# First MoE of a fused attention and two-MoE kernel: products a and b of eight slices by seven products per 2x2 blocks, g by HBM, first output as a stage of its own

## The chip, the cores and the metric

The kernel runs on one core of a Trainium2 chip. The metric is the device time of one execution in microseconds (us). Engines are called TensorE, VectorE, ScalarE, GpSimd and SyncE; profile rows abbreviate them as PE (PEld for its weight loads), DVE, ACT, POOL and SP.

## What is computed

Attention without softmax, over 4 batches, 8 heads, 576 positions and 64 dimensions, then two MLPs over the 2304 tokens. Inputs of the MLPs' weights are float64.

```python
kv = einsum('bhsd,bhse->bhde', k, v)
o = einsum('bhsd,bhde->bhse', q, kv)
x = o / sqrt(mean(o * o, -1) + 1e-6) * g_norm          # as x: [2304, 512]
a, b = x @ w_a, x @ w_b                                # [512, 1536] each
x = (a * b) @ w_out                                    # [1536, 512]
h = x @ w_in                                           # [512, 1024]
sm = softmax(h); solu = h * sm
out = (layernorm(solu) * g_ln) @ w_out2                # [1024, 512]
```

## The kernel before

Every large matrix product is made of three TensorE matmuls in the type fp32r: a value is split into a high part and a low part (the rest), and high x high, high x low and low x high are summed in PSUM. `three` (L778 to L781) issues these for a, b and the last output. A float64 weight chunk of 128 x 512 comes in as integer bits, and `decode` (L328) makes a high and a low float from it: one operation on ScalarE (L339), five on VectorE (L342 to L360), then in `store` a cast on ScalarE (L441), a subtraction (L442) and a sum (L443) on GpSimd.

The kernel is written as a program that runs its own clock: the class `Order` holds for each engine when it comes free, each operation has an assumed duration, and the main loop at the end takes at each point the TensorE work that is ready. The order of the instructions on every engine, SyncE's DMA queue included, comes out of this and is fixed when the kernel is built. All DMAs are issued by SyncE and wait there in that order.

Attention (`att_kv`, `att_1`, `att_2`, `att_hop`) makes 18 tiles of 128 tokens of x, transposed and split into xh and xl. Tiles 0 to 11 are transposed by TensorE, tiles 12 to 17 by VectorE and a trip through HBM. Between its pieces TensorE already works on the first MoE.

The first MoE goes slice by slice: 1536 hidden units are 12 slices f of 128. For each slice and each block of tokens (`BLOCKS`: 384, 384, 512, 512, 512; `EARLY` for slice 0, with two blocks of 256) `ab_items` issues 24 matmuls (a and b, four pieces of the 512 inputs, three matmuls each), ScalarE copies a out of PSUM (L833), VectorE multiplies (L834), and the product g is split (L835, L836). `y_items` then multiplies g with that slice of w_out (12 matmuls a block, L864), and the result is added into ya in SBUF on VectorE (L877; for slice 0 copied by ScalarE, L875). A weight stays in SBUF from its decode to its last use.

The second MoE's first product h is made of seven products for each 2x2 blocks instead of eight (`run_h`, `SEQ`): sums of blocks of w_in (`sums`) and of ya (`make_a`) are formed, and the seven results are combined in PSUM. Six of the seven operand pairs of one half of w_in go to HBM and come back (`late_loads`) when xh and xl are no longer needed. The softmax, the norm and the last output follow (`post_h`, `run_t`, `run_o`). SBUF comes from tile pools that are opened and released as stages end; PSUM has three pairs of banks for the MoE and two single banks for attention, which become a fourth pair when it ends.

Of the kernel before, what the change touches and what calls it, by code (L numbers as in the profile page):

```python
# [26 lines left out]
NB = 384  # L27
BLOCKS = [(0, 384), (384, 384), (768, 512), (1280, 512), (1792, 512)]
NBLK = len(BLOCKS)
EARLY = [(0, 384), (384, 256), (640, 256), (896, 384), (1280, 512), (1792, 512)]  # L30


def blocks_of(f):
    return EARLY if f < 1 else BLOCKS

HALVES = [1280, 1024]
NTT = NT // P
SC = 4
CH = 512

# [11 lines left out]
class Order:  # L52

    def __init__(self):
        self.now, self.events, self.seq = 0.0, [], 0
        self.free = {"A": 0.0, "V": 0.0, "G": 0.0}
        self.pool = 0.0
        self.end, self.cold = 0.0, 3.6  # L60
        self.dma = 1.68

    def chain(self, ops, rank=0, t=None):


# [3 lines left out]
    def until(self, t):  # L69

        while self.events and self.events[0][0] <= t:
            due, rank, seq, i, ops = heapq.heappop(self.events)
            eng, dur, fn = ops[i]
            both = eng == "S"
# [22 lines left out]
    def soon(self, eng, t, rank):  # L97

        for due, r, _, i, ops in self.events:
            if r > min(rank - 0.4, 1):  # L100
                continue
            for e, dur, _ in ops[i:i + 4]:
                if due >= t + self.AHEAD[eng]:
                    break
                if e and (e == eng or e == "S" and eng in "VG"):
                    return True
# [15 lines left out]
    def wait(self):  # L122

        assert self.events, "nothing left that anything could wait for"
        self.now = max(self.now, self.events[0][0])
        self.until(self.now)

# [7 lines left out]

# [15 lines left out]

@with_exitstack
def attention_moe_moe_kernel(ctx: ExitStack, tc, kv_in, kv_tail, q_in, g_norm, w1, w_in, w_out2, g_ln, out):
# [4 lines left out]
    INF = float("inf")  # L158

    cst = ctx.enter_context(tc.tile_pool(name="cst", bufs=1, side="left"))  # L160
    xs = ctx.enter_context(tc.tile_pool(name="xs", bufs=1, side="left"))
    wp = ctx.enter_context(tc.tile_pool(name="wp", bufs=6, side="right"))
    psm = ctx.enter_context(tc.tile_pool(name="psm", bufs=1, space=bass.MemoryType.PSUM))

    ctx.enter_context(tc.manual_schedule())

    att = tc.alloc_tile_pool(name="att", bufs=2, side="left")
    psa = tc.alloc_tile_pool(name="psa", bufs=2, space=bass.MemoryType.PSUM)
    yp = tc.alloc_tile_pool(name="yp", bufs=1, side="right")
    ph1 = tc.alloc_tile_pool(name="ph1", bufs=2, side="right")  # L170
    dr = ctx.enter_context(tc.tile_pool(name="dr", bufs=1, space=bass.MemoryType.DRAM))
    w2 = ph2 = psx = None
# [4 lines left out]
    ps_free = {0: 0.0, 1: 0.0, 2: 0.0}  # L177
    att_left = [NTT]
    started = set()

    def ps_ready():
        return min(ps_free.values())

    def ps_tile(nm):
        i = min(ps_free, key=ps_free.get)
        assert ps_free[i] < INF
        ps_free[i] = INF
        pool = psx if i == 3 else psm
        return i, pool.tile([P, 2, 512], F32, tag=f"ps{i}", name=nm)

    def ps_done(i):
        def done(t):
            ps_free[i] = t

        return (None, 0, done)


    ident = cst.tile([P, P], F32, tag="ident", name="ident")
    gn = cst.tile([P, 1], F32, tag="gn", name="gn")
    gl_sb = cst.tile([P, NF2], F32, tag="gln", name="gln")  # L200
# [1210 lines left out]
```

## Time and profile before

| | |
|---|---|
| median of 3 runs | 686.88 us (686.8 to 687.05) |
| span of the profiled execution, first to last instruction | 685.0 us |
| the profiled execution's own time | not recorded apart from its span |
| TensorE (PE) busy | 671.6 us, 98% |
| VectorE (DVE) busy | 515.3 us, 75% |
| ScalarE (ACT), GpSimd (POOL) busy | 278.8 and 279.0 us, 41% each |
| moved by DMA | 82.42 MB, mean 120 GB/s |

Matmuls are pipelined: one of 512 columns is listed with some 390 ns from its start to its end, while the next starts some 230 ns after it. So listed lengths of matmuls must not be added up; what a stream costs is read from the distance of starts, or from the merged stretches in the chain of work that ended last, which counts each stretch of time once. For the other engines the listed length of an operation is what it holds the engine. "x12" is a count, "idle before" is the time for which the engine had stood still.

### The profile page before, as it was taken

The numbers are of one execution on the slowest core, as the hardware profiler recorded it, in microseconds if no ns is written. First come the engines' busy times: TensorE is split into PE (matmuls) and PEld (weight loads), VectorE is DVE, ScalarE is ACT, GpSimd is POOL, SyncE is SP. The second block draws the span as 40 slices with busy tenths as digits, with TensorE's granted clock in tenths as the row PEclk, the third lists the DMA queues.
The fourth block names the chain that finished last, engine by engine and source line by source line (L and its number), as shares of the span: only waits on it lengthen the run. The fifth ranks groups of instructions, "written<-read, shape, count | busy, mean of one in ns | idle before, by whom it ended". The sixth has DMA issues, their size and how long they took to land.

```text
span 685.0 us, 9642 instructions
## 1 busy us (share of the span) xinstructions
PE 671.6 (98%) x3566; PEld 585.4 (85%) x3566; DVE 515.3 (75%) x752; ACT 278.8 (41%) x485; POOL 279.0 (41%) x280
## 2 busy tenths in 40 slices
PE   5999999999999999999999999999999999999998
PEld 4899988989898898989898988889787888888887
DVE  2987955888987899788888888655569969787640
ACT  3877434333233232322323323212257566654431
POOL 1669614242365454533224141311457667552010
PEclk9999999999999999999999999999999999999999
DMA  9983621122233121023041321113413564633451
GB/s 328 375 282 108 191 71 62 62 96 89 93 125 121 62 92 62 32 92 124 32 149 66 115 101 62 63 61 125 173 72 105 146 176 119 198 114 105 138 177 47
DMA packets 63694, 82.42 MB, mean 120 GB/s; under 512 B 6176, under 2 KB 45344, under 8 KB 63648
## 3 DMA queue, kind: packets, MB, share of 16 engines
q1 hardware_dynamic: 63648, 81.81, 36.0%
q8 instruction: 28, 0.46, 0.3%
q14 instruction: 18, 0.15, 0.1%
HBM read 59.25 MB, written 22.54 MB: 119 GB/s over the span
## 4 chain that ended last, share of the span: by engine, by line
PE 95%; DMA 2%; DVE 1%; SPq 1%; issue 0%; ACT 0%; ACTq 0%
PE y L864 21%; PE ab L779 15%; PE ab L781 15%; PE ab L780 14%; PE h L1027 12%; PE out L781 5%; PE out L780 5%; PE out L779 5%; PE o L657 2%; DMA kv<-in_kv 1%; DMA q<-in_q 1%; PE pkv L612 1%; PE t L756 1%; SPq L282 0%; DVE ya L877 0%
## 5 line engine op out<-in xcount | busy, mean ns | idle before, releaser
L779 PE MATMUL ab<-xh,wh_w 128*128 128x512 f32 (+2 forms) x488 | 179.5, 368 | 0.2 <-DVE ya L877 0.2
L781 PE MATMUL ab<-xh,wl_w 128*128 128x512 f32 (+2 forms) x488 | 178.4, 366 | 0.0
L780 PE MATMUL ab<-xl,wh_w 128*128 128x512 f32 (+2 forms) x488 | 178.3, 365 | 0.0
L877 DVE TENSOR_TENSOR ya<-y,ya 128x1024 f32<-128x1024 f32 (+1 forms) x110 | 122.2, 1111 | 2.7 <-PE y L864 2.5
L833 ACT COPY a<-ab 128x512 f32<-128x512 f32 (+2 forms) x61 | 32.8, 538 | 191.2 <-PE ab L781 191.2
L442 POOL TENSOR_TENSOR f_w<-f_w,wh_w 128x512 f32<-128x512 f32 x34 | 45.4, 1335 | 158.6 <-ACT wh_w L441 100.8
L779 PEld LDWEIGHTS ab<-xh,wh_w 128*128 128x128 f32 x488 | 91.8, 188 | 12.2 <-DVE ya L877 0.5
L834 DVE TENSOR_TENSOR ab<-ab,a 128x512 f32<-128x512 f32 (+2 forms) x61 | 38.8, 637 | 83.2 <-ACT a L833 83.0
L780 PEld LDWEIGHTS ab<-xl,wh_w 128*128 128x128 f32 x488 | 91.7, 188 | 11.3
L781 PEld LDWEIGHTS ab<-xh,wl_w 128*128 128x128 f32 x488 | 91.7, 188 | 10.9
L864 PE MATMUL y<-gl,wh_w 128*128 128x512 f32 (+2 forms) x244 | 89.2, 366 | 0.3 <-DVE gl L836 0.3
L864 PE MATMUL y<-gh,wh_w 128*128 128x512 f32 (+2 forms) x244 | 89.2, 366 | 0.0
L864 PE MATMUL y<-gh,wl_w 128*128 128x512 f32 (+2 forms) x244 | 89.2, 366 | 0.0
L1027 PE MATMUL h<-wd,lateh 128*128 128x512 f32 x216 | 58.0, 389 | 0.0
L443 POOL TENSOR_TENSOR wl_w<-f_w,u_w 128x512 fp32r<-128x512 f32 x36 | 47.1, 1312 | 16.0 <-DVE f_w L442 12.3
L864 PEld LDWEIGHTS y<-gl,wh_w 128*128 128x128 f32 x244 | 45.8, 188 | 6.4 <-DVE gl L836 0.7
L864 PEld LDWEIGHTS y<-gh,wh_w 128*128 128x128 f32 x244 | 45.9, 188 | 5.8 <-issue 0.2
L864 PEld LDWEIGHTS y<-gh,wl_w 128*128 128x128 f32 x244 | 45.8, 188 | 5.4
L1027 PEld LDWEIGHTS h<-wd,lateh 128*128 128x128 f32 x216 | 40.6, 188 | 8.4
L1027 PE MATMUL h<-latel,lateh 128*128 128x512 f32 x162 | 45.8, 391 | 0.7 <-ACT bt L1054 0.7
L957 POOL TENSOR_TENSOR lateh<-ya,lateh 128x512 fp32r<-128x512 f32 (+1 forms) x18 | 19.7, 1105 | 63.6 <-ACT lateh L956 63.5
L780 PE MATMUL out<-wl_o,dh 128*128 128x512 f32 (+1 forms) x114 | 43.1, 378 | 0.0
(118 smaller groups left out, 1155.1 us busy)
## 6 DMA issues: line engine op xcount, KB each, us to landing
raw_w<-in_w SPq DMA_DIRECT2D x36, 512.0 KB, 3.4
su<-ya SPq DMA_DIRECT2D x34, 256.0 KB, 2.7
kv<-in_kv SPq DMA_DIRECT2D x16, 512.0 KB, 7.6
ya<-su SPq DMA_DIRECT2D x32, 256.0 KB, 3.1
out<-ot SPq DMA_DIRECT2D x17, 256.0 KB, 2.1
raw_i<-in_w_in SPq DMA_DIRECT2D x8, 512.0 KB, 3.4
raw_o<-in_w_out SPq DMA_DIRECT2D x8, 512.0 KB, 3.2
so<-raw_o SPq DMA_DIRECT2D x8, 512.0 KB, 2.8
```

Source lines behind the costliest of these rows:

```text
L442: ("S" if k[1] == 0 and k[2] < 2 else "T", 0.62 if k[1] == 0 and k[2] < 2 else 1.32, lambda: (nc.vector if k[1] == 0 and k[2] < 2 else nc. ...
L443: ("T", 1.38, lambda: nc.gpsimd.tensor_tensor(out=lo, in0=f, in1=u, op=ALU.add)),
L657: nc.tensor.matmul(ps[m * w:(m + 1) * w, p * P:(p + 1) * P], lhsT=src[:, m * w:(m + 1) * w], rhs=bds[b % 2][:, p], start=True, stop=True)
L779: nc.tensor.matmul(o, lhsT=ah, rhs=bh, start=first, stop=False)
L780: nc.tensor.matmul(o, lhsT=ah, rhs=bl, start=False, stop=False)
L781: nc.tensor.matmul(o, lhsT=al, rhs=bh, start=False, stop=last)
L833: ("A", 0.45 * k, lambda: nc.scalar.copy(out=a, in_=ps[:, 0, 0:nb])),
L834: ("V", 0.54 * k, lambda: nc.vector.tensor_tensor(out=g, in0=g, in1=a, op=ALU.mult)),
L864: nc.tensor.matmul(o, lhsT=x[:, s], rhs=y, start=f == fs[0] and n == 0, stop=f == fs[-1] and n == 2)
L877: op = ("V", 0.9 * nb / NB, lambda: nc.vector.tensor_tensor(out=dst, in0=src, in1=dst, op=ALU.add))
L957: ("G", 2.15 * cost, lambda: nc.gpsimd.tensor_tensor(out=lo[:, n], in0=src, in1=hi[:, n].bitcast(F32), op=ALU.subtract)),
L1027: nc.tensor.matmul(o, lhsT=x, rhs=y, start=first and k == m == 0, stop=k == 1 and m == 2, skip_group_check=not first)
```

## The change

- a and b: slices 0 and 1 as before, but in blocks of 384 tokens. The others are taken in pairs of slices and pairs of blocks (`step_items`): seven products of 256 x 256 hidden-and-input blocks for a and seven for b, each of 6 matmuls of 384 columns, with sums of x blocks (`x_sum_of`) and of weight blocks (`sums_w`), and additions in and behind PSUM. The pair of slices 2 and 3 is done plainly, but in the same frame (`plain_step`, `PLAIN_STEPS`). These steps begin when all tiles of x are there. TensorE picks the first ready one of the next four products (`LOOK`).
- Weights of the pairs are split and stored to HBM as soon as they are decoded (`to_hbm`), and each group is loaded into its one fixed place when its predecessor there has been used last (`w_fill`). Slices of w_out go to HBM too and are loaded when the blocks of x in their place are used up.
- g is stored to HBM unsplit (`store_g`), 72 stores.
- The first output is a stage of its own behind all of a and b (`c_items`): for each block of tokens g is loaded (60 loads), split by ScalarE and VectorE, and all 12 slices are summed in PSUM; ScalarE copies the sum to ya. The additions at L877 are gone.
- The operands of w_in need no trip to HBM any more; w_in and w_out2 are decoded in the first output's stage.
- Some splits and sums may run on VectorE or GpSimd ("X"), whichever the build-time clock has free.
- SBUF is laid out by fixed addresses (`Map`) in place of pools, and PSUM is taken by single banks in the pair steps.

```diff
+TB = 384
+NTB = NT // TB
+PLAIN = 2
...
+            if eng == "X":
+                can = [e for e in "VG" if self.free[e] <= due + 0.01 and not self.soon(e, due, rank)]
...
+class Map:
+    XB, T0, R2, W, DEC, STG, WS, AB, CST = 0, 73728, 92160, 137216, 165888, 186368, 194560, 202752, 211968
...
+    def to_hbm(key, n, fill, then, t, rank=5):
...
+                d = w_hbm[key] = dr.tile([P, 2, n], F32, tag="hb_" + "_".join(map(str, key)), name="hb_" + "_".join(map(str, key)))
+                nc.sync.dma_start(out=d, in_=tile_.bitcast(F32))
...
+                return [
+                    add(a[:, 0:h], w1_[:, 0:h], w1_[:, h:], ALU.add), add(a[:, h:], a[:, 0:h], w0[:, 0:h], ALU.subtract),
+                    (None, 0, group(1, a, part)),
+                    add(b[:, 0:h], w0[:, 0:h], w1_[:, 0:h], ALU.subtract), add(b[:, h:], w0[:, h:], a[:, h:], ALU.subtract),
...
+    PLAIN_STEPS = {(1, 0), (1, 1), (1, 2)}
...
+    def w_fill():
+        seen = set()
+        for key in list(w_next):
+            _, m, g = key
+            at = m, (0, 1, 2, 3, 2)[g]
+            if at not in seen and slot_free.get(at, INF) <= od.now and w_in_hbm.get(key, INF) <= od.now:
+                o = wt[m][at[1]]
+                nc.sync.dma_start(out=(o if g < 4 else o[:, :, 0:CH // 2]).bitcast(F32), in_=w_hbm[key])
...
+    def store_g(f, j, s):
...
+            nc.sync.dma_start(out=g_hbm[f][:, j * TB:(j + 1) * TB], in_=g_t[s])
...
+    def x_sum_of(t):
...
+            return ("V", 0.95, lambda: nc.vector.tensor_tensor(out=o, in0=a, in1=b, op=op))
+        def both(n, src):
+            hi, lo = b12 if n == T4 else [a[t][:, (T1, T2, T3).index(n)] for a in (th, tl)]
+            return [("A", 0.82, lambda: nc.scalar.copy(out=hi, in_=src)), add(lo, src, hi, ALU.subtract),
...
+                add(t1, b21[0], t2, ALU.subtract), add(t1, t1, b21[1], ALU.add), *both(T4, t1),
+                add(t2, t2, b11[0], ALU.subtract), add(t2, t2, b11[1], ALU.subtract), *both(T3, t2)], rank=rank, t=w)
...
+            add(t1, b12[0], b11[0], ALU.subtract), add(t1, t1, b12[1], ALU.add), add(t1, t1, b11[1], ALU.subtract),
+            *both(T1, t1), add(t2, b22[0], t1, ALU.subtract), add(t2, t2, b22[1], ALU.add), *both(T2, t2), (None, 0, rest),
...
+    WSEQ = [("P1", 0, 0, B11), ("P6", 1, 1, T2), ("P2", 0, 1, B21), ("P5", 1, 0, T1), ("P7", 2, 0, T3),
+            ("P3", 2, 1, B22), ("P4", 3, 0, T4)]
...
+        def item(m, name, g, c, n):
...
+                else:
+                    w = max(w, st.get({"P2": "s1", "P7": "u2", "P3": "s5", "P4": "v"}[name], INF))
...
+                for k in range(2):
+                    sl = slice(c * 256 + k * P, c * 256 + (k + 1) * P)
+                    w = wt[m][g]
+                    three(o, w[:, 0, sl], w[:, 1, sl], x[2 * k], x[2 * k + 1], first and k == 0, k == 1, not first)
...
+        return [item(m, *p) for p in WSEQ for m in range(2)]
...
+    c_units = [(j, f) for j in range(NBLK) for f in range(NF1)]
...
-                if f < 1:
-                    op = ("A", 0.75 * nb / NB, lambda: nc.scalar.copy(out=dst, in_=src))
-                else:
-                    op = ("V", 0.9 * nb / NB, lambda: nc.vector.tensor_tensor(out=dst, in0=src, in1=dst, op=ALU.add))
...
+    ab = [[ab_items(f, j) for j in range(NTB)] for f in range(PLAIN)]
+    steps = [(plain_step if (fp, t) in PLAIN_STEPS else step_items)(fp, t) for fp in range(PLAIN // 2, NF1 // 2) for t in range(NTB // 2)]
+    b_items = [x for s in steps for x in s]
+    ATT, LOOK = 2.0, 4
...
+        if not plain and not att_left[0] and b_items:
+            n = next((n for n, x in enumerate(b_items[0:LOOK]) if x[1]() <= od.now), None)
...
+        if len(b_items) < 3 and c_items and c_items[0][1]() <= od.now:
```

## Rows read from the trace of the kernel before

**Rows 1.** The page's busy shares, and the chain's shares by line.
```profile
PE 671.6 (98%) x3566; PEld 585.4 (85%) x3566; DVE 515.3 (75%) x752; ACT 278.8 (41%) x485; POOL 279.0 (41%) x280
by line: PE y L864 21.0%; PE ab L779 14.6%; PE ab L781 14.5%; PE ab L780 14.5%; PE h L1027 12.3%; PE out L781 4.8%; PE out L780 4.8%; PE out L779 4.8%; PE o L657 2.5%; DMA kv<-in_kv 1.2%; DMA q<-in_q 1.1%; PE pkv L612 0.8%; PE t L756 0.6%; 
```

**Rows 2.** Busy time by stage: stretch, length, engines in the order PE to POOL, clock, DMA.
```profile
12.30:30.00 17.70, 16.49 (x185) 14.79 (x186) 14.22 (x26) 12.86 (x29) 10.84 (x7) 1.00 1.05 383
30.00:93.00 63.00, 62.78 (x547) 59.25 (x546) 54.06 (x105) 41.40 (x85) 39.88 (x27) 1.00 0.61 202
93.00:496.00 403.00, 402.67 (x1938) 353.82 (x1937) 314.37 (x446) 121.69 (x216) 142.78 (x110) 1.00 0.25 87
496.00:685.00 189.00, 185.06 (x842) 153.84 (x840) 129.00 (x170) 99.61 (x148) 84.78 (x129) 1.00 0.43 128
130.00:325.00 195.00, 195.00 (x948) 172.51 (x947) 166.95 (x232) 60.42 (x108) 85.98 (x65) 1.00 0.26 92
```

**Rows 3.** Chain pieces of TensorE (start, us): 512, 512, 384 columns; counts of two forms.
```profile
118.25 2.72 PE y L864 x12
125.15 2.76 PE y L864 x12
139.66 2.10 PE y L864 x12
...
L779 PE MATMUL ab<-xh,wh_w 128*128 128x512 f32 x280 | 109.2, 390 | 0.2 <-DVE ya L877 0.2
L779 PE MATMUL ab<-xh,wh_w 128*128 128x384 f32 x192 | 65.3, 340 | 0.0
```

**Rows 4.** TensorE's groups by form in 0 to 93 us, first line of three.
```profile
L779 PE MATMUL ab<-xh,wh_w 128*128 128x384 f32 x32 | 11.6, 362 | 0.0
L779 PE MATMUL ab<-xh,wh_w 128*128 128x512 f32 x16 | 6.5, 404 | 0.2 <-DVE ya L877 0.2
L864 PE MATMUL y<-gh,wh_w 128*128 128x384 f32 x16 | 5.5, 346 | 0.0
L779 PE MATMUL ab<-xh,wh_w 128*128 128x256 f32 x16 | 5.1, 316 | 0.0
L864 PE MATMUL y<-gh,wh_w 128*128 128x256 f32 x8 | 2.4, 295 | 0.0
```

**Rows 5.** VectorE's last operation on x tiles: ns min/median/max, first and last start.
```profile
L736 DVE SCALAR_TENSOR_TENSOR xl<-ya,gn,xh x24: 326/342/353, 74.3 to 92.2; 128x128 fp32r<-128x128 f32 x24
```

**Rows 6.** DMA issues: count, KB each, median us to landing.
```profile
kv<-in_kv SPq DMA_DIRECT2D x16, 512.0 KB, 7.6
si<-wd SPq DMA_DIRECT2D x6, 512.0 KB, 2.6
latel<-si SPq DMA_DIRECT2D x6, 512.0 KB, 4.6
```

**Rows 7.** Operations by line, ns min/median/max; the last row as in rows 3.
```profile
L342 DVE TENSOR_SCALAR u_w<-u_w x36: 413/418/1509, 9.5 to 440.6; 128x512 f32<-128x512 f32 x36
L345 DVE TENSOR_SCALAR u_w<-u_w x36: 395/420/1471, 9.9 to 441.0; 128x512 uint32<-128x512 uint32 x36
L351 DVE SCALAR_TENSOR_TENSOR f_w<-raw_w,u_w x36: 639/682/1662, 10.4 to 441.5; 128x512 uint32<-128x512 uint32 x36
L356 DVE TENSOR_SCALAR u_w<-f_w x36: 378/417/1411, 11.1 to 442.2; 128x512 uint32<-128x512 uint32 x36
L360 DVE SCALAR_TENSOR_TENSOR u_w<-raw_w,u_w x36: 676/692/1781, 11.6 to 442.7; 128x512 f32<-128x512 uint32 x36
L442 DVE TENSOR_TENSOR f_w<-f_w,wh_w x2: 682/686/691, 12.9 to 21.4; 128x512 f32<-128x512 f32 x2
L443 POOL TENSOR_TENSOR wl_w<-f_w,u_w x36: 1267/1298/1580, 13.7 to 447.2; 128x512 fp32r<-128x512 f32 x36
L877 DVE TENSOR_TENSOR ya<-y,ya x110: 937/1212/1226, 75.4 to 495.9; 128x1024 f32<-128x1024 f32 x66, 128x768 f32<-128x768 f32 x44
L834 DVE TENSOR_TENSOR ab<-ab,a 128x384 f32<-128x384 f32 x24 | 13.5, 563 | 25.3 <-ACT a L833 25.2
```

More of the change, by code (lines that the diff above doesn't have):

```diff
@@ L450, in attention_moe_moe_kernel, with done @@
-    waiting, waiting_i = [], []
+        if x < PLAIN and y < 2:
+            at = wt[y][2 * x]
+            hi, lo = at[:, 0], at[:, 1]
+            def done(t):
+                w_ready["w", x, y] = t
+                free()
+            od.chain([
+                ("A", 0.58, lambda: nc.scalar.copy(out=hi, in_=f)),
+                ("X", (0.62, 1.32), lambda e: tt(e)(out=f, in0=f, in1=hi.bitcast(F32), op=ALU.subtract)),
+                ("T", 1.38, lambda: nc.gpsimd.tensor_tensor(out=lo, in0=f, in1=u, op=ALU.add)),
+                (None, 0, done),
+            ], rank=rank_of(k) - 0.01, t=t)
+            return
@@ new lines, in post, with x_sums @@
+            od.chain([(None, 0, when_ok((A_S, G_S), ops))], t=od.now + 0.62)
+            plain_done.add((f, j))
+        return [(COST[TB], lambda m=m, kt=kt: ready(m, kt), lambda m=m, kt=kt: run(m, kt)) for m in range(2) for kt in range(NP)]
+    x_sum = {}
+    sum_q = list(range(3))
+    SUM_RANK = (4.5, 4.6, 4.7)
+    def x_sums():
+        if len([1 for k in w_in_hbm if k[0] == PLAIN // 2]) < 6:
+            return
+        for t in list(sum_q):
+            if any(block_ready(j) > od.now for j in (2 * t, 2 * t + 1)):
+                continue
+            if t == 1 and kv_left[0] or t == 2 and att_left[0] or t and (t - 1, T3) not in x_sum:
+                continue
+            sum_q.remove(t)
+            x_sum_of(t)
@@ new lines, in attention_moe_moe_kernel, with c_loads @@
+    s_free = [0.0] * 4
+    steps_left = {}
+    GI, GS = Slots(6), Slots(3)
+    c_units = [(j, f) for j in range(NBLK) for f in range(NF1)]
+    c_load = list(c_units)
+    g_ready, wo_at = {}, {}
+    y_ready = {}
+    def c_loads():
+        for f in range(NF1):
+            t = f // 6
+            if f not in wo_at and steps_left.get((NF1 // 2 - 1, t)) == 0 and w_in_hbm.get(("wo", f), INF) <= od.now:
+                nc.sync.dma_start(out=wo[f].bitcast(F32), in_=w_hbm["wo", f])
+                wo_at[f] = od.load(8 * CH * P)
+        if any(steps_left.get((NF1 // 2 - 1, t)) != 0 for t in range(2)):
+            return
+        while c_load and GI.ok():
+            j, f = c_load[0]
+            t0, nb = BLOCKS[j]
+            if max(g_at.get((f, i), INF) for i in range(t0 // TB, (t0 + nb - 1) // TB + 1)) > od.now:
+                return
+            c_load.pop(0)
+            s = GI.take()
+            nc.sync.dma_start(out=gi_t[s][:, 0:nb], in_=g_hbm[f][:, t0:t0 + nb])
+            at = od.load(4 * nb * P)
+            c_wait.append((j, f, s, nb, at))
+            od.chain([(None, 0, c_split)], rank=0.5, t=at)
@@ new lines, in attention_moe_moe_kernel, with c_split, done @@
+    c_wait = []
+    def c_split(t):
+        while c_wait and GS.ok() and c_wait[0][4] <= t:
+            j, f, s, nb, _ = c_wait.pop(0)
+            sg = GS.take()
+            g, (gh, gl) = gi_t[s][:, 0:nb], [a[:, 0:nb] for a in gs_t[sg]]
+            k = nb / CH
+            def done(w, j=j, f=f, s=s, sg=sg, gh=gh, gl=gl):
+                GI.give(s)
+                g_ready[j, f] = (w, gh, gl, sg)
+            od.chain([
+                ("A", 0.08 + 0.5 * k, lambda g=g, gh=gh: nc.scalar.copy(out=gh, in_=g)),
+                ("V", 0.08 + 0.54 * k, lambda g=g, gh=gh, gl=gl: nc.vector.tensor_tensor(
+                    out=gl, in0=g, in1=gh.bitcast(F32), op=ALU.subtract)),
+                (None, 0, done),
+            ], rank=0.5, t=t)
@@ L979, in h_new @@
         i = todo_h[0] // 2 if todo_h else None
-        if i not in a_ops or sum(t <= od.now for t in ps_free.values()) < places or i - 1 not in z_done:
+        if i not in a_ops or sum(place_time(n) <= od.now for n in range(4)) < places or i - 1 not in z_done:
             return INF
@@ L1115, in go @@
             if i in ON_PE:
[L1116 removed]
+                to_pe = ot_t
                 minus = [("A", 1.15, lambda h=h: nc.scalar.activation(
@@ L1245, in next_ab @@
             return busy[0]
-        two = [f for f in range(NF1) if ab[f]][0:2]
+        two = [f for f in range(PLAIN) if ab[f]][0:2]
         for n, f in enumerate(two):
```

879 lines of the change are left out of this document (569 added, 310 removed).

## Prediction

> **What bounds the kernel now.** I read the page's busy shares first, then the table by stage, then the chain of work that ended last, and only then prices of single instructions. TensorE is busy 671.6 of 685.0 us [rows 1]. The reader is to see in the stage table that this is no average over unlike stages: from 30 us on TensorE is busy in 62.78 of 63.00, 402.67 of 403.00 and 185.06 of 189.00 us, with a granted clock of 1.00 (full speed, 2.4 GHz) [rows 2]. Of the 13.4 us that it is idle, about 8.9 lie before 30 us, where kv loads arrive, and 4 in the last stage. The chain agrees: a and b have 14.6 + 14.5 + 14.5 = 43.6% of it, y 21.0% [rows 1]. So only fewer or shorter matmuls can save much, and whatever else the change adds counts only where TensorE comes to wait for it.
>
> **TensorE: what goes.** Chain share times span is the present cost of a and b: 0.436 x 685.0 = 298.7 us. Piece by piece the same comes out. Twelve matmuls of 512 columns take 2.72 to 2.76 us (0.2267 to 0.230 each), twelve of 384 take 2.10 (0.175) [rows 3]; a 256 one, scaled by columns from the 384, is an estimated 0.117. a and b have 3 x 280, 3 x 192 and 3 x 16 of these [rows 3, 4]: 840 x 0.2283 + 576 x 0.175 + 48 x 0.117 = 298.2.
>
> After the change every a/b matmul has 384 columns. Slices 0 and 1, and the pair 2, 3 in all three of its steps, stay plain: 4 slices x 6 blocks x 24 matmuls = 576. The eight slices 4 to 11 are 4 pairs x 3 pairs of blocks x 14 products (seven for a, seven for b) x 6 matmuls = 1008, where 1152 would be plain. 1584 x 0.175 = 277.2 us. Gain: 298.7 - 277.2 = 21.5 us, and up to 24 at 0.1734, an estimate from the faster row of 512 columns less 128 columns at 2.4 GHz (0.2267 - 0.0533). So the change shortens 7/8 of two thirds of a and b, and gives almost nothing back by the narrower blocks: per column 0.456 ns against 0.446. The first output has 720 matmuls where y had 732: 432 x 0.2283 + 288 x 0.175 = 149.0 for 149.2 us, 0.2 less. h and the last output keep their matmuls.
>
> So TensorE's part alone: 685.0 - 21.5 - 0.2 = 663.3 us of span.
>
> **Attention stage (to 93 us).** The last x tile is written at about 92.5 us [rows 5]. Until then TensorE fills the gaps with 96 a/b matmuls of 384 columns, 46 of 512, 48 of 256, and 48 and 24 y matmuls of 384 and 256 (each row of [rows 4] stands for three lines of its kind): 16.8 + 10.5 + 5.6 + 8.4 + 2.8 = 44.1 us. After the change nothing but slices 0 and 1 may run there (no y, no pair step before the last tile), and their blocks 0 to 4: 10 x 24 x 0.175 = 42.0 us; block 5 waits for the last tile. That leaves 2.1 us uncovered: 0 if attention gets shorter by it, 5 if blocks arrive in lumps. I take 2.1.
>
> **Weights by HBM.** Before, a decoded weight stays in SBUF. Now each group of a pair, and each w_out slice, is stored and loaded again, all on SP's queue, with g beside it (72 stores, 60 loads). Bytes while a and b run: 22 MB weights out, 16 back, 14 of g out, 14 raw in: 66 MB in some 237 us, 280 GB/s; the queue reached 383 [rows 2]. A 512 KB store lands after 2.6 us, a load after 4.6, and a load in the saturated start after 7.6 [rows 6]. A step lasts 14 x 1.05 = 14.7 us, and a group's place is free some 8 to 9 us before its successor is needed (group 0: used in products 1 and 5 of the row of seven, needed at the next step's first). So I cost the reload at nothing; the cover is the remaining products of the step. Were a load to take 12 us, four changes of pair would wait about 3 us each: 12 us. Behind a waiting store on SP stand the other stores and these loads.
>
> **VectorE and GpSimd (93 to about 330 us).** Removed: 110 adds into ya (122 us in all, 0.95 to 1.22 each [rows 7]); in their place 10 copies on ScalarE. Added and kept, by the medians of [rows 7]:
> - 28 of the 36 weight decodes (eight done by then; the code's limit for the attention stage is nine) x (0.418 + 0.420 + 0.682 + 0.417 + 0.692 = 2.63) = 74 us, and 28 joins on GpSimd x 1.30 = 36
> - sums of x: 3 x 13 operations of 768 columns with both inputs in SBUF; the nearest row has 512 columns and 0.686, so 1.03 each, 40 us
> - weight splits and sums, where 256 columns count half of 512: 8 x (3 x 0.686 + 5 x 0.343) + 2 x (0.686 + 2 x 0.343) + 12 x 0.686 = 41 us if all on VectorE, twice that on GpSimd (1.30 against 0.686)
> - 12 steps x 10 additions and products x 0.563 = 68, plain ones 14 x 0.563 = 8
>
> That is 231 us of 237 if GpSimd takes none of the 41, 190 (80%) if it takes all. VectorE at 167 of 195 us (86%) held TensorE up nowhere in 130 to 325 us [rows 2], so pressure of this size is bearable. But the place of a wait is new. Within a step a's products need each other's evictions: product 4 of the seven waits for an addition on VectorE that waits for product 7, with three other products between the two, 3.15 us; less 0.563 for the addition and an estimated 0.4 for hand-overs that is some 2.2 us of slack. A VectorE operation in the way costs 0.4 to 1.0, or 1.5 to 1.8 at its longest. Bounds for the twelve steps: 0 (slack never used up) to 12 us (1 us each). I take 1.5 in all, nearer to the row without waits.
>
> One thing speaks against this. Among the rows the decode operations on SBUF show medians of 0.418 and 0.692 but longest cases of 1.509 and 1.781, while the ya adds, which have one input in PSUM, never pass 1.226 [rows 7]; the excess is about one GpSimd operation. The Trainium skill (SBUF — State Buffer, "SBUF: two separate sides") says that VectorE operations with two SBUF inputs or in a fast mode share a port pair with GpSimd under an exclusive lock, the later one blocked for the whole instruction. The trace agrees, and the sums of x are of the blocked kind where the ya adds were not; what that gives is the first rival.
>
> **Hand-overs.** The first output begins only when the products are through; its g loads and w_out loads are released one step (14.7 us) earlier, against 4.6 us a load. The second MoE's weights are decoded during 149 us of first output, their sums stay in SBUF now. Its second A operand waits for the last first-output unit, then GpSimd's four sums of 256 columns and splits of 3.5 x 512, (2 + 3.5) x 1.30 = 7.2 us [rows 7], under 14 x 3 x 0.2283 = 9.6 us of the first pair. I cost both at nothing, with 0 to 3 us each in the range.
>
> **Sum.** 663.3 + 2.1 + 1.5 = 666.9 us of span. The median of the runs stands 686.88 - 685.0 = 1.9 above the profiled span; the change leaves what lies around the span alone: 668.8, forecast **669**.
>
> **Rivals.**
> 1. The lock and the load together: sums and decodes on VectorE cannot run beside GpSimd. 231 + 36 = 267 us in a row would be 30 too many. Against it, 76 us of VectorE's work reads PSUM and can lie beside GpSimd, and 40 us (w_out's decodes and splits) may slip into the first output. So I let 40% of the 30 reach TensorE, 12 us: **681**, between 675 and 685. It shows as TensorE waiting for weight loads whose stores waited for the joins. Chance 0.19.
> 2. Slower: the product chain of a step is exposed. The price is one wait per step at products 4 and 7. A gain of 21.7 - 2.1 = 19.6 us over 12 steps is used up at 1.63 us per step; together with the 2.2 us of slack the addition must be late by 3.8 us, three long cases of [rows 7] in a row. At 2 us per step and a load that misses its place at each of four changes (3 us): 663.3 + 2.1 + 24 + 12 + 1.9 gives **703**; just beyond the border, 689. Against it: VectorE was 86% busy before without one such wait, and its operations that read PSUM show no long cases. Chance 0.10; within the border 0.03.
> 3. Full gain: attention ends earlier, since VectorE loses four ya adds and the splits of g in 62 to 93 us, and no step waits: **665**, down to 662.5. Chance 0.10.
> That the diff does less than it says is excluded by counting its products; that only 8 of 12 slices change is in the sum.
>
> **How the numbers follow.** Forecast case (665 to 675): 0.58. Faster by over 0.2% (about what a measurement of this kernel can tell from no change) is 0.58 + 0.19 + 0.10 = 0.87; same 0.03; slower 0.10. The range goes from 662.5 (24 us gained, no wait) to 682, inside rival 1; beyond it lie 0.13 and a part of rival 1, and little below.
>
> **What would show it.** Right: TensorE has 120 more a/b matmuls and 12 fewer of y's place, and is busy some 20 us less; idle time between 60 and 110 us of about 2 us; the steps' products back to back, 6 matmuls in 1.05 us; VectorE about 80 to 85% in the pair steps. Wrong: TensorE waiting on VectorE at every step (rival 2), on weight loads (rival 1), 384-column matmuls slower than 0.175 us, or a first output that starts with a gap.

## The result, and the profile after

The changed kernel takes 675.44 us (median; 673.4 to 675.92), the kernel before 686.96 us beside it: a ratio of 0.9822, 95% interval 0.9805 to 0.9839. That is 11.5 us less, where 17.9 were forecast. The profiled execution took 673.4 us with a span of 671.6, 13.4 us less than the span before; it is the fastest of the four executions, and the median lies 2.0 us above it.

The page of the changed kernel: busy time and instructions of each engine, the chain's shares by engine and by line, and of the DMA issues the loads of weight groups (count, KB each, median us to landing).

```profile
PE 650.2 (97%) x3674; PEld 594.9 (89%) x3674; DVE 534.6 (80%) x774; ACT 317.2 (47%) x571; POOL 332.3 (49%) x319
PE 84%; DMA 6%; DVE 5%; issue 2%; POOL 2%; SPq 1%; ACT 0%; DVEq 0%; POOLq 0%; ACTq 0%
PE ps L1372 20%; PE ps L982 16%; PE ps L984 16%; PE ps L983 16%; PE ps L1514 13%; DMA wt<-hb 2%; PE ps L867 2%; DVE t L1079 1%; DMA raw<-in_w 1%; DMA kv<-in_kv 1%; PE ps L965 1%; DMA hb<-stg 1%; PE ps L821 1%; DVE f L441 1%; POOL r L897 1%
wt<-hb SPq DMA_DIRECT2D x26, 512.0 KB, 6.3
```

TensorE is busy 21.4 us less than in [rows 1], which is the size of the forecast gain, but the span fell by only 13.4. So TensorE now stands still for longer. The chain has DMA 6% and VectorE 5% in it, where a, b, y and the outputs of TensorE had nearly all. A load of a weight group lands after 6.3 us; 4.6 were taken from [rows 6].

Busy time of the changed kernel by stage (stretch; length, PE, PEld, DVE, ACT, POOL; granted clock, DMA share, GB/s). Lines 1 and 2 are attention and the first two slices, lines 3 to 6 mostly the pairs of slices, line 7 the first output and line 8 the rest.

```profile
0.00:30.00 30.00, 20.42 (x251) 18.01 (x252) 17.95 (x34) 16.88 (x39) 12.09 (x14) 1.00 0.96 351
30.00:93.00 63.00, 61.37 (x531) 59.68 (x531) 57.45 (x106) 35.35 (x78) 42.96 (x29) 1.00 0.74 254
93.00:145.00 52.00, 52.00 (x302) 52.00 (x302) 51.44 (x58) 18.60 (x34) 35.11 (x26) 1.00 0.71 251
145.00:190.00 45.00, 39.29 (x207) 36.97 (x207) 44.15 (x63) 18.55 (x36) 25.72 (x18) 0.96 0.63 226
190.00:290.00 100.00, 100.00 (x579) 100.00 (x578) 91.35 (x145) 44.88 (x91) 56.40 (x48) 1.00 0.87 314
290.00:333.20 43.20, 42.65 (x247) 42.33 (x246) 27.83 (x50) 16.64 (x34) 11.38 (x9) 1.00 0.99 360
333.20:483.40 150.20, 149.42 (x727) 131.87 (x726) 116.70 (x155) 64.83 (x109) 61.62 (x44) 1.00 0.63 208
483.40:671.60 188.20, 185.01 (x843) 154.06 (x842) 127.75 (x169) 101.42 (x152) 87.04 (x133) 1.00 0.40 121
...
156.00:158.00 2.00, 0.15 (x1) 0.16 (x2) 2.00 (x3) 1.63 (x4) 0.34 (x1) 1.00 0.77 190
158.00:162.00 4.00, 4.00 (x16) 4.00 (x17) 4.00 (x9) 0.43 (x2) 0.00 (x0) 0.65 1.02 403
```

The reader is to see one stage that differs from its neighbours. In 145 to 190 us TensorE is busy 39.29 of 45.00 us and its clock is 0.96. Behind it, the same kind of steps run for 100 us without a gap. VectorE is busy 51.44 of 52.00 and 44.15 of 45.00 us from 93 to 190 us, 98 to 99%, and 91% after that; the page's 80% hides this. The last two lines show the worst place: 2 us in which TensorE does one matmul, and 4 us behind it at 0.65, part of them at the lower clock of 1.2 GHz (16 matmuls, where 23 fit at 2.4 GHz). A matmul usually starts 0.173 us after the one before it: 579 lie in the 100.00 us of line 5. The gaps over this distance sum to 7.0 us in 145 to 190 us. Behind the longest, 11 matmuls start some 0.32 us apart, at half clock, which adds 1.6 us, and the first starts behind each gap add some 0.6: 9.2 us in all.

What TensorE waited for in 93 to 345 us of the changed kernel (us in total, times, longest):

```profile
PE ps L982 <- ACT s L1248: 2.7, 1, 2.7
PE ps L982 <- DVE a L1207: 1.4, 2, 1.1
PE ps L982 <- ACT stg L624: 0.6, 1, 0.6
PE ps L982 <- DMA wt<-hb: 0.6, 1, 0.6
...
```

The longest is put down to ScalarE: it copies a product out of PSUM (L1248) that the third product of the row needs. Lines picked from the timeline just before it show why ScalarE was late (start, length, engine and operation, in brackets the idle time before it and what ended it):

```profile
150.91 2.00 POOL L626 TENSOR_TENSOR stg<-ws,stg 128x512 fp32r<-128x512 f32 x1
151.80 1.92 DVE L1079 TENSOR_TENSOR t<-t,xl 128x768 f32<-128x768 f32 x1
154.32 0.68 DVE L450 SCALAR_TENSOR_TENSOR u<-raw,u 128x512 f32<-128x512 uint32 x1
155.08 1.26 POOL L588 TENSOR_TENSOR f<-f,u 128x512 f32<-128x512 f32 x1 [2.17 <-DVE u L450]
156.37 0.67 ACT L429 ACTIVATE u<-raw 128x512 f32<-128x512 f32 x1 [1.35 <-POOL f L588]
157.31 0.86 ACT L1248 COPY s<-ps 128x384 f32<-128x384 f32 x2
157.85 0.44 PE L982 MATMUL ps<-xh,wt 128*128 128x384 f32 x1 [2.68 <-ACT s L1248]
```

Read it upwards. The copy stands behind a decode operation on ScalarE (L429), which waited for GpSimd's join (L588), which waited for the last decode operation on VectorE (L450). That one stood behind a sum of x (L1079), which took 1.92 us instead of 0.94, beside a GpSimd operation that took 2.00. So a VectorE that is late holds TensorE up by way of two other engines whose order is fixed.

### The profile page after: what moved, and what is told of

Same layout as the page of the kernel before. It is cut to its first block, busy times and chain, and to the rows that moved or that the text cites. A ratio compares the mean times of both kernels' runs of the same rounds, so it can differ in the third digit from the quotient of the medians.

```text
span 671.6 us, 10623 instructions
## 1 busy us (share of the span) xinstructions
PE 650.2 (97%) x3674; PEld 594.9 (89%) x3674; DVE 534.6 (80%) x774; ACT 317.2 (47%) x571; POOL 332.3 (49%) x319
## 4 chain that ended last, share of the span: by engine, by line
PE 84%; DMA 6%; DVE 5%; issue 2%; POOL 2%; SPq 1%; ACT 0%; DVEq 0%; POOLq 0%; ACTq 0%
PE ps L1372 20%; PE ps L982 16%; PE ps L984 16%; PE ps L983 16%; PE ps L1514 13%; DMA wt<-hb 2%; PE ps L867 2%; DVE t L1079 1%; DMA raw<-in_w 1%; DMA kv<-in_kv 1%; PE ps L965 1%; DMA hb<-stg 1%; PE ps L821 1%; DVE f L441 1%; POOL r L897 1%
## 5 line engine op out<-in xcount | busy, mean ns | idle before, releaser
L1372 PE MATMUL ps<-gh,wo 128*128 128x512 f32 (+1 forms) x480 | 137.6, 367 | 0.0
L982 PE MATMUL ps<-xh,wt 128*128 128x384 f32 x384 | 130.6, 340 | 5.3 <-ACT s L1248 2.7
L983 PE MATMUL ps<-xl,wt 128*128 128x384 f32 x384 | 128.9, 336 | 1.6 <-DVE xl L945 1.6
L984 PE MATMUL ps<-xh,wt 128*128 128x384 f32 x384 | 128.8, 335 | 0.0
L1372 PEld LDWEIGHTS ps<-gh,wo 128*128 128x128 f32 x480 | 88.7, 188 | 11.1
L1372 PE MATMUL ps<-gl,wo 128*128 128x512 f32 (+1 forms) x240 | 88.3, 368 | 0.8 <-DVE gl L1346 0.8
L1514 PE MATMUL ps<-bo,ao 128*128 128x512 f32 x378 | 87.2, 389 | 0.0
L982 PEld LDWEIGHTS ps<-xh,wt 128*128 128x128 f32 x384 | 72.3, 188 | 7.4 <-ACT s L1248 3.0
L983 PEld LDWEIGHTS ps<-xl,wt 128*128 128x128 f32 x384 | 72.3, 188 | 2.0 <-DVE xl L945 1.9
L984 PEld LDWEIGHTS ps<-xh,wt 128*128 128x128 f32 x384 | 72.3, 188 | 0.0
L588 POOL TENSOR_TENSOR f<-f,u 128x512 f32<-128x512 f32 x32 | 45.9, 1434 | 52.1 <-DVE u L450 52.1
L983 PE MATMUL ps<-gw,dh 128*128 128x512 f32 (+1 forms) x152 | 57.4, 378 | 0.0
L982 PE MATMUL ps<-gw,dh 128*128 128x512 f32 (+1 forms) x152 | 57.4, 378 | 0.0
L429 ACT ACTIVATE u<-raw 128x512 f32<-128x512 f32 x52 | 35.1, 674 | 38.7 <-POOL f L588 25.7
L982 PE MATMUL ps<-th,wt 128*128 128x384 f32 x144 | 48.8, 339 | 1.0 <-DMA wt<-hb 0.6
L984 PE MATMUL ps<-th,wt 128*128 128x384 f32 x144 | 48.5, 337 | 0.0
```

Of the source, the lines that this page charges most:

```text
L429: nc.scalar.activation(out=u, in_=w[:, :, 1].bitcast(F32), func=AF.Abs)
L588: od.chain([("T", 1.32, lambda: nc.gpsimd.tensor_tensor(out=f, in0=f, in1=u_t[su], op=ALU.add)), (None, 0, have)], rank=rank_of(k), t=t)
L982: nc.tensor.matmul(o, lhsT=ah, rhs=bh, start=first, stop=False, skip_group_check=skip)
L983: nc.tensor.matmul(o, lhsT=ah, rhs=bl, start=False, stop=False, skip_group_check=skip)
L984: nc.tensor.matmul(o, lhsT=al, rhs=bh, start=False, stop=last, skip_group_check=skip)
L1372: nc.tensor.matmul(o, lhsT=x, rhs=y, start=f == 0 and n == 0, stop=f == NF1 - 1 and n == 2)
```

## The experiments

The sums of x are 39 VectorE operations of 768 columns with both inputs in SBUF. How long they take in the changed kernel (ns min/median/max, first and last start):

```profile
L1079 DVE TENSOR_TENSOR t<-t,xl x15: 941/1026/1923, 99.5 to 181.7; 128x768 f32<-128x768 f32 x15
L1079 DVE TENSOR_TENSOR tl<-t,th x9: 946/962/1622, 104.5 to 184.9; 128x768 fp32r<-128x768 f32 x9
L1079 DVE TENSOR_TENSOR t<-xh,t x6: 944/1536/1928, 106.4 to 173.4; 128x768 f32<-128x768 f32 x6
L1079 DVE TENSOR_TENSOR t<-xh,xh x3: 946/1700/2043, 97.4 to 157.7; 128x768 f32<-128x768 f32 x3
...
L1207 DVE TENSOR_TENSOR a<-ps,s x24: 541/546/558, 167.7 to 331.3; 128x384 f32<-128x384 f32 x24
L588 POOL TENSOR_TENSOR f<-f,u x32: 1265/1320/1936, 55.7 to 311.7; 128x512 f32<-128x512 f32 x32
```

And the stage view for this line alone (stretch, length, VectorE's busy time and count, clock, DMA share, GB/s):

```profile
93.00:200.00 107.00, 49.51 (x39) 0.98 0.68 240
```

Their total is 49.51 us: 1.27 each, where the shortest take 0.94 and 1.03 was forecast. The additions with an input in PSUM (L1207) stay between 541 and 558 ns. My theory was therefore: load and lock (VectorE and GpSimd blocking each other) on VectorE in 93 to 190 us cost the 9 us; the rivals were the order of work on VectorE, and the DMA queue.

**All pairs plain.** Does anything but the seven products bring time?

```diff
-    PLAIN_STEPS = {(1, 0), (1, 1), (1, 2)}
+    PLAIN_STEPS = {(fp, t) for fp in range(1, 6) for t in range(3)}
...
-    sum_q = list(range(3))
+    sum_q = []
```

> The changed kernel with all fifteen pair steps done plainly (eight products for seven, 1728 a/b matmuls of 384 columns for 1584), and so without the sums of x and of weights; weights and g still go by HBM and the first output is still a stage of its own. Theory (the gain is TensorE's saved matmuls, and the first pair steps lose some 9 us to VectorE's load): 144 more matmuls x 0.172 = 24.8 us more, 8 to 9 us of waits between 145 and 190 us gone: 671.6 + 16 = 688 us of span, about 690 us, no gain over the kernel before; no wait of TensorE on VectorE between 145 and 190 us. Rival (the gain comes from what else was changed: no additions into ya, no operands of w_in by HBM): stays below 680 us.

Measured: 689.4 us, ratio 1.0032 (1.0014 to 1.0051). TensorE's busy time is 672.9 us. The stage row of this kernel:

```profile
145.00:190.00 45.00, 45.00 (x262) 45.00 (x261) 37.43 (x60) 16.68 (x33) 21.45 (x16) 1.00 0.85 294
```

So the whole gain is that of the seven products; the rest of the change (trips to HBM, the stage for the first output, blocks of 384, the new layout) together costs 0.3%. With VectorE at 37.43 of 45 us there is no gap here.

**Thin sums of x.**

```diff
+            if o is a:
+                o, a, b = (v[:, :, 0:48] for v in (o, a, b))
```

> The changed kernel in the same order of instructions, but the 21 of 39 sums of x that add in place take 48 of their 384 columns per row (the other columns are left out of the sum). VectorE has some 21 x 0.8 = 17 us less to do, GpSimd the same. Theory (VectorE is late with the sums of x, at 100% busy from 93 to 200 us): TensorE's waits between 145 and 190 us, 7 us and more with the low clock behind them, fall to under 2 us, span about 663 to 665 us. Rival (ScalarE's fixed order or weight loads are what is late there): the waits stay within 2 us of what they are, span 669 us or more.

Measured: 665.78 us, ratio 0.9687 (0.9671 to 0.9703). Its stage row, and then the sums that were thinned (48 columns of each of two pieces, so 128x96):

```profile
145.00:190.00 45.00, 45.00 (x262) 45.00 (x261) 42.05 (x66) 21.52 (x42) 25.79 (x23) 1.00 0.68 238
...
L1081 DVE TENSOR_TENSOR t<-t,xl x15: 243/324/1235, 98.5 to 172.9; 128x96 f32<-128x96 f32 x15
...
L1081 DVE TENSOR_TENSOR t<-t,xh x3: 243/875/877, 124.9 to 171.6; 128x96 f32<-128x96 f32 x3
```

The edit reaches 18 of the 39 sums, not the 21 that I counted. Every gap of this stage is gone and the clock stays at 1.00, though only 16.9 us went from VectorE's busy time (534.6 to 517.7) and nothing was taken off the queue. A wait of 1.2 us for a weight load at 101 us, ahead of the stage, is new. So VectorE's lateness is the cause; this doesn't yet tell load from lock.

**Thin joins on GpSimd.** Here VectorE's own work is left as it is.

```diff
-        od.chain([("T", 1.32, lambda: nc.gpsimd.tensor_tensor(out=f, in0=f, in1=u_t[su], op=ALU.add)), (None, 0, have)],
+        od.chain([("T", 1.32, lambda: nc.gpsimd.tensor_tensor(out=f[:, 0:64], in0=f[:, 0:64], in1=u_t[su][:, 0:64], op=ALU.add)), (None, 0, have)],
```

> The changed kernel in the same order, but GpSimd's 32 joins of high and low weight part take 64 of 512 columns (the rest of the weights' lower part is left out). VectorE's own work stays as it is; GpSimd has 32 x 1.1 = 35 us less. Lock theory (operations with inputs in SBUF on VectorE and GpSimd block each other, 12 us of excess in the 39 sums alone): VectorE's busy time falls by 10 to 30 us though nothing was taken from it, the mean of the 39 sums comes from 1.27 to under 1.15 us, and the waits at 145 to 190 us fall below 3 us: span 664 to 667 us. Rival (VectorE has simply too much to do): its busy time falls by under 5 us and the waits stay, span 669 us or more.

Measured: 668.09 us, ratio 0.9726 (0.9711 to 0.9741). The page's busy shares of this kernel:

```profile
PE 648.2 (97%) x3674; PEld 593.7 (89%) x3674; DVE 513.8 (77%) x774; ACT 317.9 (48%) x571; POOL 298.1 (45%) x319
```

Its stage row, and then the total of its sums of x:

```profile
145.00:190.00 45.00, 43.80 (x250) 42.84 (x249) 43.86 (x65) 20.16 (x40) 23.39 (x22) 1.00 0.63 226
...
93.00:200.00 107.00, 45.06 (x39) 1.00 0.74 264
```

VectorE has the same 774 operations and is busy 20.8 us less, with GpSimd busy 34.2 us less. That is what a lock between the two does. The gaps of the stage fall from 7.0 to 1.6 us. The sums give only 4.5 of the 20.8 us: 1.155 us each, where below 1.15 was expected; the rest is other VectorE operations, which got shorter too. The joins are also a link of the chain above, which gets shorter with them; this run can't part the two.

**Every g store twice.** Is the queue's cover as wide as the prediction had it?

```diff
+            if f not in g_two:
+                g_two[f] = dr.tile([P, NT], F32, tag=f"g2{f}", name=f"gn{f}")
+            nc.sync.dma_start(out=g_two[f][:, j * TB:(j + 1) * TB], in_=g_t[s])
```

> The changed kernel with each of the 72 stores of g made twice, the second time to a tensor that nobody reads: 14 MB more on the queue, most of it between 60 and 335 us. Theory of the prediction (trips by HBM are covered by the products in between): within 2 us of the changed kernel. Rival (the queue is nearly full, 319 to 359 GB/s between 200 and 332 us against 387 at most, so the cover is about used up): TensorE waits for weight loads from 200 us on, 5 to 12 us longer.

Measured: 682.08 us, ratio 0.992 (0.9893 to 0.9946), so 6.6 us more than the changed kernel. Two waits of TensorE in this kernel (us in total, times, longest):

```profile
PE ps L982 <- DMA wt<-hb: 3.5, 3, 1.6
PE ps L1375 <- DVE gl L1349: 3.0, 5, 0.8
```

Three stretches of this kernel:

```profile
190.00:245.00 55.00, 54.12 (x311) 53.51 (x310) 50.03 (x77) 24.34 (x50) 33.56 (x29) 1.00 0.97 338
245.00:290.00 45.00, 45.00 (x262) 45.00 (x261) 37.50 (x66) 19.80 (x40) 23.95 (x19) 1.00 1.00 377
290.00:345.00 55.00, 53.56 (x307) 52.92 (x306) 32.22 (x58) 19.32 (x39) 14.94 (x12) 1.00 1.03 381
```

14 MB more fill the queue (0.97 to 1.03 share) and are paid for. The rival was right that there is no margin, but the price is hardly a wait for weight loads: these are 3.5 us, against 0.6 in the changed kernel's first profile and 3.2 in the next run, which is the same kernel again. Most of it, 4.9 us, is the first output, which took 154.9 us against 150.0; there g's split comes late (L1349).

**The changed kernel again**, unaltered, as a control for the runs that follow.

> The changed kernel unaltered, as the measure for the three beside it on the same chip: 675 us, ratio to the kernel before 0.982; TensorE's waits between 145 and 190 us some 6 us.

Measured: 675.26 us, ratio 0.9827 (0.9814 to 0.9841). Its profiled execution (675.56 us, span 673.7) is nearer to the median than the first one: 7.1 us of gaps and some 11 matmuls at half clock in 145 to 190 us, 1.4 us of gaps before the first output. TensorE's longest entry in 93 to 345 us is another one than before:

```profile
PE ps L982 <- DMA wt<-hb: 3.2, 2, 1.9
```

The 1.9 us, a wait for a weight load, end at 152.2 us; the load was issued at 147.4 and landed at 152.1. Just before it SyncE, whose order is fixed, had stood at a store of g behind a product on VectorE (L1146), as it did four times and for 10 us in all between 136 and 153 us. In the first profile two waits put down to L624 and L1079 (0.6 and 0.4 us) also end 0.14 us behind the landing of a weight load. So the same lateness of VectorE reaches TensorE by loads as well as by ScalarE. Whether issuing these loads ahead of the g stores would help was not tried.

**Sums of x planned as locked.** The planner of the order now counts them as operations that may not start while a GpSimd operation runs. This changes the order of work and, but for two operations that move from GpSimd to VectorE, none of the work.

```diff
-            return ("V", 0.95, lambda: nc.vector.tensor_tensor(out=o, in0=a, in1=b, op=op))
+            return ("S", 0.95, lambda: nc.vector.tensor_tensor(out=o, in0=a, in1=b, op=op))
```

> The changed kernel with one letter changed: the sums of x are ordered as operations that may not run beside GpSimd (the kind that the decodes already have), so that every engine gets another order with the same work. Theory (VectorE and GpSimd have more than fits before the first output, the lock included): the time stays within 3 us of the changed kernel, and what is gained at 145 to 190 us (4 us or more of TensorE's 6 us of waits) comes back as a wait for slices of w_out in the first block of the first output, near 325 to 360 us. Rival (only the order was bad, the work would fit): 664 to 668 us.

Measured: 676.93 us, ratio 0.9855 (0.9841 to 0.9868). TensorE's longest wait behind 93 us, and the stage row:

```profile
PE ps L1372 <- DMA wo<-hb_wo: 4.5, 1, 4.5
```

```profile
145.00:190.00 45.00, 42.03 (x239) 40.81 (x237) 44.32 (x64) 20.26 (x40) 25.68 (x18) 1.00 0.65 235
```

The gaps of the stage halve (3.6 us), but w_out's slices are now late for the first output, where TensorE waits 4.5 us at 341 us, 10 us after its start. This order doesn't win the time; it moves the wait to what was put off.

**The pair of slices 4 and 5 plain too.** Less work in the stage for 36 more matmuls.

```diff
-    PLAIN_STEPS = {(1, 0), (1, 1), (1, 2)}
+    PLAIN_STEPS = {(1, 0), (1, 1), (1, 2), (2, 0), (2, 1), (2, 2)}
```

> The changed kernel with the pair of slices 4 and 5 plain as well, so that seven products begin one pair (50 us) later: 36 more a/b matmuls x 0.172 = 6.2 us more for TensorE, fewer sums of weights, and 44 us more time for the sums of x. Theory (VectorE is late only because the sums of x are due within 55 us of the end of attention): waits and low clock at 145 to 190 us, 7 to 9 us, are gone; 671.6 + 6.2 - 8 = 670 us of span, 671 to 673 us in all, 2 to 4 us faster than the changed kernel. Rival (VectorE is late whenever seven products start): the same waits 50 us later, 680 us.

Measured: 675.37 us, ratio 0.9841 (0.9817 to 0.9866): no gain over the changed kernel. Its stage rows:

```profile
145.00:190.00 45.00, 45.00 (x261) 45.00 (x260) 43.50 (x51) 15.55 (x29) 27.12 (x21) 1.00 0.71 275
190.00:245.00 55.00, 52.63 (x293) 50.20 (x293) 54.25 (x78) 23.10 (x46) 27.03 (x20) 1.00 0.66 236
```

The gaps and the low clock leave 145 to 190 us, and 3.4 us of gaps come back at 190 to 245, where VectorE is now busy 54.25 of 55.00 us. The 6.2 us of matmuls eat the rest. Neither the 671 to 673 us of the theory nor the 680 of its rival came.

The edit did not give the sums of x 44 us more, as I had it. The later sums of a pair of blocks write over blocks of x, so the code holds them back (`rest`) until the plain steps have read these. The sums of this kernel alone (stretch, length, VectorE's busy time and count, clock, DMA share, GB/s):

```profile
111.00:165.50 54.50, 1.54 (x1) 1.00 0.87 308
165.50:230.00 64.50, 37.72 (x32) 1.00 0.56 205
```

The one in the first line began at 110.7 us: in the 54.5 us that were won no sum starts, and VectorE does decodes there instead (9 of L432 in 93 to 145 us, where the changed kernel has 4). 32 of the 39 sums moved behind together with the products that need them.

**Both together.** Its edit is the two diffs above.

> Both easings together: the planner counts the sums of x as operations that exclude GpSimd, and the pair of slices 4 and 5 is done plainly as well (36 matmuls of 384 columns more, 36 x 0.172 = 6.2 us). Measured so far: the changed kernel 675.3 us with 7.0 us of TensorE gaps and about 2 us of half clock in 145 to 190 us; the sums alone planned as locked 676.9; the pair alone 675.4, with the gaps moved to 190 to 245 us. Theory (VectorE is late because of load and lock together, so the gaps go only when both are eased): no gap over 1 us between 145 and 333 us, 675.3 + 6.2 - 9 = 672 to 674 us. Rival (VectorE is full in any order, what is eased in one stretch comes back in the next): gaps of 3 us or more in all after 190 us, 675 to 678 us.

Measured: 676.5 us, ratio 0.9855 (0.9838 to 0.9871). TensorE's longest wait behind 93 us, and the stage rows:

```profile
PE ps L983 <- DVE tl L1079: 3.0, 1, 3.0
```

```profile
145.00:190.00 45.00, 45.00 (x261) 45.00 (x260) 40.74 (x57) 15.68 (x28) 24.32 (x16) 1.00 0.78 284
190.00:245.00 55.00, 51.35 (x289) 50.49 (x288) 52.27 (x76) 24.27 (x46) 23.34 (x18) 0.98 0.66 232
```

The rival's number came: 4.6 us of gaps between 230 and 245 us, now on a sum of x itself, with the clock low behind them. Its reason, that VectorE is full in any order, isn't shown: from 93 to 190 us VectorE is busy 48.41 of 52 and 40.74 of 45 us, so 7.9 us are free, while 32 sums are held back here too. What the three runs show is that these edits move the wait and beat nothing; an order that does the sums before decodes, or that keeps the old blocks of x so that sums needn't wait, was not tried.

**The addition ahead of product 4 made late.** This prices the second rival: in the steps of slices 8 and 9 two VectorE operations more stand before it, in those of 10 and 11 five more.

```diff
-                return [("V", VT, lambda: nc.vector.tensor_tensor(out=o, in0=ps, in1=s, op=ALU.add)), *free, *then,
+                def add_late():
+                    for _ in range({4: 2, 5: 5}.get(fp, 0) if i == 3 else 0):
+                        nc.vector.tensor_scalar(out=ps, in0=ps, scalar1=1.0, scalar2=None, op0=ALU.mult)
+                    nc.vector.tensor_tensor(out=o, in0=ps, in1=s, op=ALU.add)
...
+                return [("V", VT, add_late), *free, *then,
```

> The changed kernel; in the steps of the slices 8 and 9 the addition that product 4 waits for is made late by two more VectorE operations on the same PSUM place (times 1.0, some 0.55 us each), in those of 10 and 11 by five. Prediction's slack (2.2 us between products 7 and 4, and 4.2 us for the second matrix that stands behind the first on VectorE): 1.1 us each, 3.5 us for both, cause no wait in the first three steps (under 0.5 us in all); 2.75 us each, 6.8 us for both, cause some 2.6 us a step in the last three, 8 us: 682 to 684 us. Rival (no slack: the chain is already tight there): waits of 2 us a step in the first three as well, 688 us or more. Second rival (TensorE is ahead by far more than a step's slack): no wait at all, 675 us.

Measured: 692.8 us, ratio 1.0083 (1.0069 to 1.0097), 17.6 us of span more than the control. The stretches of the steps with two and with five, and between them a wait of the third step with two, whose additions come at 291 and 293 us and so lie in the last line's stretch:

```profile
245.00:290.00 45.00, 44.26 (x255) 43.81 (x254) 39.98 (x68) 18.86 (x39) 21.41 (x18) 1.00 0.84 299
...
291.46 0.44 PE L982 MATMUL ps<-xh,wt 128*128 128x384 f32 x1 [1.02 <-DVE a L1210]
...
290.00:349.00 59.00, 49.94 (x262) 47.67 (x261) 46.13 (x83) 17.43 (x36) 14.16 (x11) 0.94 0.79 292
```

Two operations cost 0.9 us of gaps in the first step, none in the second and 1.7 in the third, where a split and three decode operations stood before the additions: 2.7 us, where under 0.5 was forecast. (The control has a gap of 1.4 us at 293 us, for a load.) So the slack was there, but other VectorE work can use it up. Five operations took 2.96 us and cost 11.1 us of gaps in the last three steps, 3.7 a step where 2.6 was forecast; 2.6 of them lie behind the start of the first output, into which the last products reach, and it took 153.9 us where 150.0 were. Some 18 matmuls at half clock behind these gaps add 2.6 us. That, and a's and g's additions being late one after the other, makes the price higher than the forecast. The time is one that the first rival allows, but its sign, 2 us in each of the first three steps, isn't there.

## Why the prediction was right, and where it was 6.4 us off

The direction and the range held, and the gain came from where the prediction put it, the matmuls that are saved. The median of 675.4 lies just above the forecast case's own 665 to 675: the range held because it took in the first rival, whose mechanism is in the runs. Of the 6.4 us, 4.7 are span (671.6 for 666.9); the rest is that the profiled execution is the fastest of the four. Term by term, with the profiled span (685.0 to 671.6):

| term of the sum | forecast | measured |
|---|---|---|
| matmuls of a and b | -21.5 (to -24) | -24.7 |
| first output | -0.2 | -0.2 |
| attention stage, to 93 us | +2.1 | +2.1 |
| waits of the steps | +1.5 (0 to 12) | +9.2 |
| reload and hand-overs | 0 | +0.7 |
| last stage | 0 | -1.1 |

The first output is 150.0 us from its first to its last matmul, less 1.0 for a last product of a and b that lies between them (149.2 before, by its matmuls). The last stage goes from the first h matmul, at 495.7 us before and 483.4 after, to the end of the span; in the control it is 189.1 us, as long as before, so this term is one of the execution. The terms add up to -14.0; 0.6 us to the -13.4 of the spans I can't assign. It was luck that the miss stayed this small: 3.2 us more gain from the matmuls hid part of 7.7 us more of waits.

- **Matmuls of a and b: sized too small.** Starts lie 0.173 us apart where nothing waits, 100.00 us for 579 in the stage table; 1584 x 0.173 = 274.0 for 298.7 us, a little beyond the prediction's upper end. Its 0.175 came from pieces of y in the chain [rows 3]; by their starts the 384-column matmuls of a and b lay 0.174 us apart (median) in the kernel before too. (The change takes two thirds of a and b to 7/8; "7/8 of two thirds" says it the wrong way round. The sum has it right.)
- **Attention stage: right in its number, not in its working.** +2.1 are 61.37 busy of 63.00 us where 62.78 were [rows 2], 1.4 us more idle, and 0.7 more before 30 us (20.42 against 21.09 us busy). 1.6 us are one wait for an x tile (L945) at 76.5 us, not for the last one. The last tile came at 87 us and not at 92.5, and 252 matmuls of a and b had started by 93 us, not 240, so 43.6 of the 44.1 us were covered. That the idle time came to 2.1 us all the same was luck.
- **Waits of the steps: the mis-sized term.** 9.2 us in 145 to 190 us, where I took 1.5. The step that failed is the pair "190 (80%) to 231 of 237 us" and "pressure of this size is bearable". The count of the work was right: GpSimd took nearly all of the 41 us of splits, and by the prediction's prices what VectorE did in 93 to 333 us is 189 us. But it was busy 51.44 + 44.15 + 91.35 + 27.83 = 214.8 of 240 us, since its operations took longer than the rows' medians. And the sum was taken over the whole of 93 to 330 us, while the sums of x fall in 97 to 185 us. By the prediction's prices the operations of 93 to 190 us are 39 x 1.03 for the sums, 9 x 2.63 for decodes, 31 x 0.563 for additions and products and 2 for splits: 83 of 97 us, 86%, the very share that the prediction called bearable. They took 95.6, 98 to 99%, and in a fixed order. So a sum by stages alone would not have shown it; the lock had to be in the prices.
- **Lock: the first rival's mechanism, with about 9 of its 12 us, mostly in other places.** It was to come as a wait for weight loads; these are 0.6 us in the first profile (1.6 with the two that end at a load's landing) and 3.2 in the control, and the longest of them was issued late behind VectorE's products, not behind joins. The rest came through the sums (1.27 us each for an expected 1.03) and ScalarE's order. The Trainium skill (SBUF — State Buffer, "SBUF: two separate sides") says that such VectorE operations and GpSimd shut each other out for a whole instruction. The runs agree: 39 sums between 0.94 and 2.04 us, GpSimd's joins between 1.27 and 1.94, additions from PSUM never over 0.56, and 20.8 us of VectorE's busy time gone with 34.2 us of GpSimd's.
- **The slack of a step: about right.** From 190 to 290 us there is no gap, and 1.1 us of delay per addition cost 0.9, 0 and 1.7 us in three steps. (Its 0.4 us for hand-overs stands in no row.) The second rival's price past the slack was too low, as the late addition shows.
- **Reload at nothing: small, but not nothing, and wrong in its margin.** Over 93 to 333 us the queue carried some 292 GB/s, near the 280 of the working; but that average hides 314 to 360 GB/s at a share of 0.87 to 0.99 in 190 to 333 us, and loads took 6.3 us, not 4.6. TensorE waited 0.6 us for them, 3.2 in the control, and 1.5 and 1.6 where joins or sums were thin. With 14 MB more the kernel took 6.6 us longer.
- **Full gain, 665 us:** the thin sums show that this is what the change gives without VectorE's lateness, 665.8, though with part of the sums left out.

## What to carry to other kernels

Average an engine's load over the stretch in which its work is due, not over the loop that it belongs to: 89% over 240 us hid 97 us at 98%, and the cost came there. And where VectorE and GpSimd both work on SBUF, add to VectorE's bill the time that GpSimd takes from it: by medians the same 97 us were 86% full. Look for it in the longest cases of VectorE's SBUF operations against those that read PSUM. Here only taking work off VectorE or GpSimd closed the gaps; three edits of order and place moved them. Before such a move is read as a full engine, check in the trace that the work could start earlier at all: two of the three held it back themselves.

## What the runs showed of the hardware that I had not expected

A gap of TensorE can cost more than its length, and not the same each time. Behind the 2.7 us wait at 155 us the granted clock was 0.65 in 158 to 162 us. At 76.5 us there is a wait of 1.6 us for an x tile in three executions (with a gap of 0.3 us just before it in the third); in the changed kernel and its control the clock in 79 to 83 us is 1.00, with every g store doubled it is 0.59. Why it fell in one and not in the others isn't shown. The row of the changed kernel:

```profile
79.00:83.00 4.00, 4.00 (x25) 4.00 (x23) 3.97 (x9) 1.03 (x3) 1.16 (x1) 1.00 0.81 238
```

The same stretch with the doubled stores:

```profile
79.00:83.00 4.00, 4.00 (x15) 4.00 (x16) 3.97 (x10) 1.52 (x4) 1.47 (x1) 0.59 0.92 303
```

Here 15 matmuls were done where 25 were in the row above: 10 x 0.173 = 1.7 us. A forecast that prices a wait by its length alone is then too low.

Taking about 34 us of work off GpSimd took about 21 us off VectorE, whose operations were all still there: at this mix of the two engines, three fifths of the GpSimd time that went had been VectorE's too.
